# One merge's PSUM bank: chunk 2's 16-row blocks take the first bank of the feed-forward sums

## The chip, the cores and the metric

The kernel runs on one core of one Trainium2 chip. The metric is the device time of one execution in microseconds (us), and the number given for a kernel is the median of its runs. TensorE (PE; its weight loads are PEld), VectorE (DVE), ScalarE (ACT) and GpSimd (POOL) each work through their own instructions in order. SyncE (SP) starts the transfers. PSUM, into which TensorE writes, has eight banks, and this kernel uses all eight while the attention runs.

## What is computed

The reference runs a recurrence over 768 time steps and then two gated feed-forward layers over all 3072 tokens of width 320. Cut to what matters:

```python
for t in range(S):                                   # S = 768, 4 batches x 8 heads, D = 40
    y[:, :, t] = einsum('bhd,bhde->bhe', rt, state)
    Sa = einsum('bhde,bhe->bhd', state, at)
    state = state * wt[:, :, None, :] - einsum('bhd,bhe->bhde', Sa, bt) + einsum('bhd,bhe->bhde', vt, kt)
x = y.transpose(0, 2, 1, 3).reshape(3072, 320)
x = (silu(x @ w_gate) * (x @ w_val)) @ w_out         # first layer, d_ff = 1536
x = (sigmoid(x @ w_gate2) * (x @ w_val2)) @ w_out2   # second layer
```

## The kernel before, in words

The recurrence is cut into 12 chunks of 64 steps. Within a chunk it becomes matrix work: products of the decayed keys, the inverse of a unit triangular matrix for each of 32 head and batch pairs, and a few products that carry the state from chunk to chunk. Each chunk m passes through these stages.

- `prep_a(m)` loads and scales the inputs, transposes them (`tr4`, L371) and makes four key products `kps` (L486), each in the bank "mm" for every chunk but 0. ScalarE takes the triangle `bn` out of `kps` (L495, L496), VectorE takes the masked rest `lq` (L498), and only then is the bank free for the next `kps`.
- `prep_b(m)` inverts the triangle. For chunks below `FEW = 3` it calls `halves` (L546): VectorE solves blocks of 16 rows (L567, L573) and transposes them (L578, L579); then TensorE merges pairs of them into blocks of 32 rows, in a PSUM tile `hps` (L588, L601), with a copy by ScalarE between the two (L596) and copies behind them (L615, L617, L619). From chunk 3 on it calls `whole` (L510): VectorE solves blocks of 32 rows by itself (L520, L521, L526, L532, L536) and a transfer through DRAM turns them. Both kinds end in the last merge, from 32 to 64 rows: `zps` and `xps` (L647) with their copies (L664, L662). The result is `X`.
- `chain(m)` carries the state: `qps` (L692 or L766), `ups` (L710 or L787, which needs `X`), `sps` (L723 or L811). For chunks 0 to 2 it runs in two halves of eight pairs, the first in the bank "qu", the second in "zy".
- `post(m)` makes the outputs: `aps` (L861), masked by VectorE (L870), and `yps` (L892), read by VectorE (L906), all of them in "zy".
- `extra(m)` runs block m of the first feed-forward layer: `split` (L1058 to L1074), `gate` into the bank "gv" (L1112), and sums into the two banks "po0" and "po1" (L1128), which ScalarE copies out (L1383).

The eight banks are two of "tp" (transposes) and one each of "zy", "qu", "gv", "mm", "po0" and "po1". A tile with a tag waits until the tile that had the tag before is read for the last time. The merges of chunk 0 and 1 (`hps`, `zps`, `xps`) have "po0" and "po1", those of all later chunks have "mm", the same bank as `kps`.

The order of the work is made in two steps. A function `merge` (L920) interleaves the stages of several chunks by written costs and due times: beside each other run `chain` and `post` of chunk m, `prep_b` of chunk m + 1, `prep_a` of chunk m + 2, the feed-forward block m - 1, and the splitting of feed-forward weights into two parts (`load_w`, L1000 to L1038, work of all engines but TensorE). Then the framework, when the kernel is built, orders the instructions of each engine by a timed plan: earlier in the program has priority, and an instruction whose tile has no free bank yet stands back. On the chip each engine keeps that order.

Two SBUF buffers matter as well. `halves` and `whole` share the tag "pr", of which there is one: in chunk 2 it holds `zt`, which ScalarE writes at L596 and TensorE reads at L601; in chunk 3 it holds `nt` (L520), the first step of the solve. The tag "sn", also one, is free by then.

After the attention the remaining feed-forward work runs as a stream on TensorE (`gates`, L1167, and `add`, L1128).

Of the kernel before, what the change touches and what calls it, by code (L numbers as in the profile page):

```python
# [24 lines left out]
FEW = 3  # L25
# [17 lines left out]
def attention(ctx, tc, st, ident, ins, banks, extra, early, more):  # L43
# [75 lines left out]
    def tied(mats, gates):  # L119
        for x, ys, c in [(mats[0], gates, "Sync"), *((x, mats[:1], "NoSync") for x in mats[1:])]:  # L120
            for y in ys:
                tc.add_manual_dep(
                    x.ins,
                    y.ins.name,
                    mybir.DependencyInfo(getattr(mybir.DependencyClass, c), mybir.DependencyReason.DATA),
                    reason="one group",
                )
# [89 lines left out]
    ptp, pzy, pqu, pmm, po = banks()  # L217
# [406 lines left out]
    def prep_b(m):  # L624
        X = xinv[m % 2]
        while m not in inv:
            yield
        bn = inv.pop(m)
        pool, tag = (po, f"po{m}") if m < 2 else (pmm, "mm")
        if m < FEW:  # L630
            ps = pool.tile([P, NS, 32], F32, tag=tag, name="hps")
            steps = halves(m, X, bn, ps)
        else:
            steps = whole(m, X, bn)
        for x1t in steps:
            yield

        zt = wk.tile([P, NS, 32], F32, tag="zt", name="zt")
        for n in range(2):
            ps = pool.tile([P, NS, 32], F32, tag=tag, name="zx"[n] + "ps")  # L640
            mats = []
            for q in range(NS):
                for h2 in range(2):
                    with group(m, not mats):
                        lo, hi = slice(64 * h2, 64 * h2 + 32), slice(64 * h2 + 32, 64 * h2 + 64)
                        mats.append(
                            nc.tensor.matmul(  # L647
                                ps[(hi, lo)[n], q],
                                lhsT=(bn[lo, q, 32:64], zt[hi, q])[n],
                                rhs=(x1t[lo, :, q], X[hi, q, 32:64])[n],  # L650
                                start=True,
                                stop=True,
                                tile_position=(64 * h2 + 32 * n, 64 * h2 + 32 - 32 * n),
                            )
                        )
            if m >= FEW:
                tied(mats, copied if n else [])
            copied = []
            for h2 in range(2):
                lo, hi = slice(64 * h2, 64 * h2 + 32), slice(64 * h2 + 32, 64 * h2 + 64)  # L660
                if n:
                    nc.scalar.mul(out=X[lo, :, 32:64], in_=ps[lo], mul=-1.0)  # L662
                else:
                    copied.append(nc.scalar.copy(out=zt[hi], in_=ps[hi]))  # L664
            yield
        if m == 0:
            marks["merged"] = mats[-1]

    def group(m, first):
        return tc.high_priority(2000) if m >= FEW and not first else nullcontext()  # L670
# [278 lines left out]
    for t, step in ((x16, 17), (xs, 34)):  # L949
        t = t.rearrange("p r t -> p (r t)")[:, ::step]  # L950
        nc.gpsimd.tensor_copy(out=t, in_=odd[:, 0:1].to_broadcast([P, 16]) if step == 34 else less.to_broadcast([P, 16]))
    nc.gpsimd.memset(tkb[2][..., D:64], 0.0)
    start = [(prep_b(0), *QB)]
    if NCH > 1:
        start.append((prep_a(1), *QA))
    merge(start)
    for m in range(NCH + 1):
        todo = []
        if m == 0:
            todo.append((early(range(NFA - 2)), *QW))  # L960
            if len(groups) > 1:
                todo.append((all_powers(), *QP))
        if m == 1:
            todo.append((early(range(NFA - 2, NFA), lambda x: behind(x, "late")), *NL))
        if 0 <= m < NCH:
            todo.append((cp(m), *(NP if m else QN)))
        if 0 <= m < NCH - 1:
            todo.append((prep_b(m + 1), *(NB if m else QC)))
        if 2 <= m + 2 < NCH:
            todo.append((prep_a(m + 2), *(NA if m else QD)))  # L970
        todo.append((ahead(m), *(NX if m > 1 else (QX, NF1)[m])))
        if more is not None:

            free = {NCH - 2: [f"lq{NCH % 3}", f"tkb{NCH % 3}"]}
            free[NCH - 1] = [f"lq{(NCH + 1) % 3}", f"tkb{(NCH + 1) % 3}", "part0"]
            free[NCH] = ["part1", f"lq{(NCH + 2) % 3}", "part3", f"tkb{(NCH + 2) % 3}", "ut", "rbd", "part2"]
            todo.append((more(free.get(m, []), (raw_of(wk, ("zt", "x1t")), (pmm, "mm")) if m >= NCH - 1 else None), *NM))
        merge(todo)
# [578 lines left out]
```

## Time and profile before

| | |
|---|---|
| median of 3 runs | 1272.05 us (1271.22 to 1274.35) |
| profiled execution, its own time | 1274.74 us |
| span of its profile, first to last instruction | 1272.7 us |
| TensorE busy | 1185.2 us, 93% |
| VectorE busy | 687.8 us, 54% |
| ScalarE busy | 592.3 us, 47% |
| GpSimd busy | 557.7 us, 44% |
| mean granted TensorE clock | 0.956 of full speed |

The profile is one execution. Its own time is 2.7 us above the median of the runs, and 2.0 us of it lie outside the span. A timeline row names start, duration, engine, line, operation, the tile written and the tiles read, and in brackets how long the engine was idle before it and whose end it waited for. Names are those of the program; "part" stands for tensors that are parts of shared buffers (`X`, `an`, `mask`, the state). The clock of TensorE has two levels here, 2.4 GHz (1.00) and 1.2 GHz (0.50); a number between them is a mean over a stretch with both. Matmuls of 32-bit numbers count as two records each.

### The profile page before, as it was taken

How to read it: one execution, taken by the hardware profiler on the slowest of the kernel's cores; microseconds unless marked ns; L12 is line 12 of the kernel's file. 1: busy time of each engine (PE TensorE's matmuls, PEld its weight loads, DVE VectorE, ACT ScalarE, POOL GpSimd, SP SyncE). 2: the span in 40 equal slices, each digit the busy share in tenths (PEclk: the TensorE clock that was granted, in tenths of full speed). 3: DMA queues.
4: the chain of work that ended last, by engine and by line, in shares of the span. 5: the costliest groups of instructions: out<-in, count | busy, mean ns of one | idle time of the engine just before them, and what ended most of it. 6: DMA issues, size and time to landing. Idle time of an engine off the chain costs nothing.

```text
span 1272.7 us, 31392 instructions
## 1 busy us (share of the span) xinstructions
PE 1185.2 (93%) x12545; PEld 1070.1 (84%) x12545; DVE 687.8 (54%) x1432; ACT 592.3 (47%) x1447; POOL 557.7 (44%) x749
## 2 busy tenths in 40 slices
PE   5598799999999999899999999999999999999997
PEld 4487588889889988788898888888888888888886
DVE  6867769876678667956867544467121212121111
ACT  8465546556655575455433433445232323232222
POOL 5744842233223224356855766676232223222221
PEclk8678868999999999999999999999999999999998
DMA  7444664544655555343464543323010101000001
GB/s 221 131 131 148 146 168 123 123 99 111 153 121 115 115 136 122 88 106 110 125 237 126 182 160 127 107 88 91 2 46 1 46 1 35 1 21 1 22 1 25
DMA packets 180460, 124.38 MB, mean 98 GB/s; under 512 B 134608, under 2 KB 160208, under 8 KB 179536
## 3 DMA queue, kind: packets, MB, share of 16 engines
q1 hardware_dynamic: 180144, 122.11, 35.5%
q8 instruction: 101, 1.65, 0.5%
q14 instruction: 55, 0.45, 0.1%
q10 hardware_dynamic: 160, 0.16, 0.1%
HBM read 90.81 MB, written 31.43 MB: 96 GB/s over the span
## 4 chain that ended last, share of the span: by engine, by line
PE 60%; DVE 22%; ACT 8%; issue 4%; DMA 2%; POOL 2%; SPq 0%; DVEq 0%; ACTq 0%; POOLq 0%
PE g L1167 31%; PE po L1128 16%; DVE pr L526 4%; PE gv L1112 4%; DVE part L532 3%; PE kps L486 2%; PE aps L861 2%; PE tp L371 2%; DVE lq L498 1%; PE ups L787 1%; ACT bn L496 1%; DVE am L870 1%; DVE dt L1015 1%; ACT bn L495 1%; ACT part L751 1%
## 5 line engine op out<-in xcount | busy, mean ns | idle before, releaser
L1167 PE MATMUL g<-x,w 128*128 128x512 f32 (+1 forms) x1792 | 419.8, 385 | 2.1 <-DVE g L1174 2.0
L1167 PEld LDWEIGHTS g<-x,w 128*128 128x128 f32 x1792 | 323.3, 188 | 62.8 <-issue 2.8
L1176 POOL TENSOR_TENSOR hl<-g,hh 128x256 fp32r<-128x256 f32 x216 | 162.1, 756 | 281.8 <-ACT hh L1175 253.9
L1174 DVE TENSOR_TENSOR g<-g,g 128x256 f32<-128x256 f32 x216 | 82.1, 419 | 342.4 <-PE g L1167 340.1
L1128 PE MATMUL po<-w,hh 128*128 128x320 f32 x1152 | 233.6, 311 | 0.9 <-ACT hh L1118 0.8
L1128 PEld LDWEIGHTS po<-w,hh 128*128 128x128 f32 x1152 | 187.0, 188 | 9.9 <-ACT hh L1118 1.0
L1175 ACT CAST hh<-g 128x256 fp32r<-128x256 f32 x216 | 86.9, 406 | 179.4 <-PE po L1128 169.7
L1112 PE MATMUL gv<-x,w 128*128 128x256 f32 x1152 | 165.6, 291 | 3.8 <-DVE g L1117 2.5
L1128 PE MATMUL po<-w,hl 128*128 128x320 f32 x576 | 151.1, 313 | 3.6 <-POOL hl L1119 3.5
L1112 PEld LDWEIGHTS gv<-x,w 128*128 128x128 f32 x1152 | 147.7, 192 | 6.8 <-DVE g L1117 3.9
L1171 ACT ACTIVATE g<-g 128x256 f32<-128x256 f32 x216 | 73.0, 382 | 149.5 <-PE g L1167 143.1
L1119 POOL TENSOR_TENSOR hl<-g,hh 128x256 fp32r<-128x256 f32 x72 | 62.8, 872 | 128.8 <-ACT hh L1118 127.9
L1032 POOL TENSOR_TENSOR dt<-dt,w 128x384 f32<-128x384 f32 (+1 forms) x72 | 80.3, 1116 | 87.5 <-ACT w L1030 42.7
L1128 PEld LDWEIGHTS po<-w,hl 128*128 128x128 f32 x576 | 99.6, 188 | 5.6 <-POOL hl L1119 5.2
L498 DVE TENSOR_TENSOR lq<-kps,part 64x256 f32<-64x256 f32 x96 | 40.5, 422 | 85.9 <-ACT bn L496 67.0
L526 DVE TENSOR_TENSOR pr<-part,sn 128x4 f32<-128x4 f32 (+4 forms) x135 | 76.2, 565 | 3.7
L1014 DVE TENSOR_SCALAR dt<-dt 128x384 int32<-128x384 int32 (+1 forms) x72 | 41.8, 580 | 52.8 <-POOL dt L1011 52.5
L486 PE MATMUL kps<-lq,kbt 104*128 104x128 f32 x384 | 61.3, 309 | 8.9 <-DVE lq L498 6.4
L532 DVE TENSOR_REDUCE part<-pr 128x2 f32<-128x4 f32 (+4 forms) x135 | 66.6, 493 | 2.8
L486 PEld LDWEIGHTS kps<-lq,kbt 104*128 104x128 f32 x384 | 53.4, 215 | 13.2 <-PE yps L892 4.1
L861 PE MATMUL aps<-rbd,ut 104*128 104x128 f32 x384 | 57.1, 295 | 6.1 <-DVE ysb L906 3.6
L1030 ACT CAST w<-dt 128x384 fp32r<-128x384 f32 (+1 forms) x72 | 35.6, 495 | 55.3 <-DVE dt L1015 48.2
(185 smaller groups left out, 1711.4 us busy)
## 6 DMA issues: line engine op xcount, KB each, us to landing
raw<-in_w_dram SPq DMA_DIRECT2D x48, 384.0 KB
xd<-x SPq DMA_DIRECT2D x12, 896.0 KB
x<-xd SPq DMA_DIRECT2D x11, 896.0 KB
raw<-in_w_dram SPq DMA_DIRECT2D x24, 320.0 KB
ld<-in_a_kb_dram SPq DMA_DIRECT2D x22, 320.0 KB
ld<-rd SPq DMA_DIRECT2D x64, 80.0 KB
pn<-pd SPq DMA_DIRECT2D x32, 160.0 KB
ld<-in_a_a_dram SPq DMA_DIRECT2D x12, 320.0 KB
```

What stands on the lines that cost most here:

```text
L486: nc.tensor.matmul(kps[:, n].rearrange("p h t -> p (h t)"), lhsT=kbt[0:PW, n, :], rhs=lq[m % 3][0:PW, 4 * g4 + n].rearrange("p h t -> p (h ...
L526: nc.vector.tensor_tensor(out=o, in0=xs[:, 0:kk, None, 0:n].to_broadcast([P, kk, 2, n]), in1=sn[:, None, n : n + 2, 0:n].to_broadcast([P, ...
L532: nc.vector.tensor_reduce(out=xs[:, 0:kk, n : n + 2], in_=o, axis=AX.X, op=ALU.add)
L861: nc.tensor.matmul(aps[:, n, h2], lhsT=ut[0:PW, x, 2 * h2 : 2 * h2 + 2].rearrange("p u s -> p (u s)"), rhs=rbd[0:PW, x, h2].rearrange("p b ...
L1032: sub(out=tf, in0=tf, in1=w.bitcast(F32), op=ALU.subtract)
L1112: nc.tensor.matmul(gv[n], lhsT=p, rhs=q, start=e == 0, stop=e == len(seq) - 1)
L1128: self.nc.tensor.matmul(ops[u], lhsT=p[:, us], rhs=q, start=first and n == 0, stop=last and n == 2)
L1167: nc.tensor.matmul(gv[k][:, 0:n], lhsT=p, rhs=cols(at), start=e == 0, stop=e == len(seq) - 1)
L1171: nc.scalar.activation(out=g[j], in_=gv[0][:, j], func=AF.Silu if silu else AF.Sigmoid)
L1174: nc.vector.tensor_tensor(out=g[j], in0=gv[1][:, j], in1=g[j], op=ALU.mult)
L1175: nc.scalar.copy(out=hh, in_=g[j])
L1176: self.heng.tensor_tensor(out=hl, in0=g[j], in1=hh.bitcast(F32), op=ALU.subtract)
```

## The change

For chunk 2 the tiles `hps`, `zps` and `xps` get the tag "po0" in place of "mm". For chunks 0 and 1 the tag is what it was ("po0", "po1"), and from chunk 3 on too ("mm"). No instruction is added, removed or altered in size.

```diff
@@ -626,7 +626,7 @@
         while m not in inv:
             yield
         bn = inv.pop(m)
-        pool, tag = (po, f"po{m}") if m < 2 else (pmm, "mm")
+        pool, tag = (po, f"po{m % 2}") if m < FEW else (pmm, "mm")
         if m < FEW:
             ps = pool.tile([P, NS, 32], F32, tag=tag, name="hps")
             steps = halves(m, X, bn, ps)
```

## Rows read from the trace of the kernel before

**Rows 1.** The page: TensorE's granted clock in 40 slices of 31.8 us, tenths.

```profile
PEclk8678868999999999999999999999999999999998
```

**Rows 2.** Windows: stretch, us, busy of PE, PEld, DVE, ACT, POOL, clock, DMA share, GB/s.

```profile
152.00:165.00 13.00, 10.63 (x68) 9.42 (x69) 5.75 (x10) 8.06 (x20) 8.09 (x11) 0.52 0.93 233
165.00:174.00 9.00, 7.04 (x220) 6.69 (x219) 5.22 (x12) 6.11 (x14) 3.01 (x4) 0.88 0.30 103
174.00:201.00 27.00, 26.49 (x438) 24.02 (x437) 21.44 (x48) 10.54 (x24) 11.96 (x17) 0.51 0.67 166
201.00:245.90 44.90, 42.32 (x695) 38.73 (x695) 41.29 (x78) 27.67 (x68) 12.81 (x15) 1.00 0.42 99
244.30:288.00 43.70, 40.55 (x674) 37.87 (x674) 32.57 (x65) 25.77 (x63) 12.49 (x15) 1.00 0.54 123
329.60:371.20 41.60, 40.17 (x672) 37.69 (x671) 30.97 (x64) 25.29 (x63) 12.26 (x15) 1.00 0.53 121
...
454.50:496.20 41.70, 40.25 (x674) 37.78 (x673) 31.06 (x64) 25.37 (x63) 12.33 (x15) 1.00 0.49 112
```

**Rows 3.** PE timeline, chunk 3's key products and chunk 2's merge.

```profile
146.60 1.16 PE L486 MATMUL kps<-lq,kbt 104*128 104x128 f32 x8
...
167.41 1.06 PE L486 MATMUL kps<-lq,kbt 104*128 104x128 f32 x8
...
171.67 1.26 PE L588 MATMUL hps<-x1t,bn 16*32 16x16 f32 x128 [1.06 <-DVE lq L498]
...
179.75 1.05 PE L601 MATMUL hps<-part,pr 32*16 32x16 f32 x102
...
189.25 1.92 PE L647 MATMUL xps<-part,zt 32*32 32x32 f32 x64
...
193.72 2.08 PE L486 MATMUL kps<-lq,kbt 104*128 104x128 f32 x8 [0.51 <-ACT part L662]
```

**Rows 4.** DVE timeline, chunk 2's blocks, then the solves of chunks 3 and 4.

```profile
138.45 0.70 DVE L578 STREAM_TRANSPOSE x1t<-x 128x512 f32<-128x512 f32 x1
...
172.97 0.61 DVE L906 TENSOR_TENSOR ysb<-yps,pn 128x320 f32<-128x320 f32 x2
...
180.92 0.85 DVE L617 TENSOR_SCALAR part<-hps 16x256 f32<-16x256 f32 x2 [0.37 <-PE hps L601]
181.80 0.69 DVE L520 TENSOR_TENSOR nt<-sn 128x512 f32<-128x512 f32 x1
182.41 0.70 DVE L619 STREAM_TRANSPOSE x1t<-part 128x512 f32<-128x512 f32 x1
...
211.28 0.71 DVE L536 STREAM_TRANSPOSE x1t<-part 128x512 f32<-128x512 f32 x1
...
218.47 1.23 DVE L512 STREAM_TRANSPOSE sn<-bn 128x1024 f32<-128x1024 f32 x1
```

**Rows 5.** Windows, columns as in Rows 2: from the end of L906 on.

```profile
173.58:181.80 8.22, 7.96 (x164) 6.97 (x164) 3.97 (x9) 1.65 (x3) 4.70 (x7) 0.50 0.52 125
...
173.60:245.90 72.30, 68.98 (x1132) 62.91 (x1133) 62.73 (x125) 38.20 (x91) 25.17 (x33) 0.81 0.51 123
...
173.60:211.30 37.70, 36.11 (x561) 32.67 (x562) 31.54 (x64) 17.77 (x44) 14.15 (x21) 0.64 0.54 136
```

**Rows 6.** ACT timeline: po0 copied out, and chunk 4's keys ready.

```profile
144.44 0.43 ACT L1383 COPY ob<-po 128x320 f32<-128x320 f32 x1
...
176.94 0.59 ACT L482 COPY kbt<-tp 104x512 f32<-104x512 f32 x1 [0.94 <-PE tp L371]
```

**Rows 7.** PE timeline: chunk 1's merge in its own bank, between chunk 2's key products.

```profile
106.05 1.16 PE L486 MATMUL kps<-lq,kbt 104*128 104x128 f32 x8
...
108.72 1.27 PE L588 MATMUL hps<-x1t,bn 16*32 16x16 f32 x128
...
120.57 1.25 PE L647 MATMUL xps<-part,zt 32*32 32x32 f32 x64
...
122.96 1.16 PE L486 MATMUL kps<-lq,kbt 104*128 104x128 f32 x8 [1.14 <-DVE lq L498]
```

## The prediction

> **What bounds the kernel now.** The table of the page says that TensorE is busy for 93% of the span. I read its clock by slices next: it is 9 tenths and more from the eighth slice (223 us) to the end, but 6 tenths in the sixth (159 to 191 us) [rows 1]. The windows by stage say more. The chunk windows are cut at the starts of `ups` (L787). From chunk 4 on a chunk takes 41.6 to 41.7 us, of which TensorE is busy 40.2 at full clock; chunk 3's stretch takes 43.7 with 40.55 [rows 2]. So TensorE bounds the later chunks, a shift of the work before them is kept to the end, and what this change can win lies between 140 and 246 us. Before that, 152 to 165 us runs at a clock of 0.52 and 174 to 201 us at 0.51, almost wholly at 1.2 GHz [rows 2].
>
> The timelines show what holds that stretch. The blocks of chunk 2 are solved and transposed (L578) at 139.15 us [rows 4], yet their merge starts at 171.67, 32.5 us later, and the row names the reader of a key product, L498, as what it waited for [rows 3]. That is the shared bank: the four products of chunk 3 pass through "mm" from 146.60 to 168.5 us, and the merge gets it behind the last of them. Behind the merge's last copy, L662, the first product of chunk 4 starts at 193.72 [rows 3], though its keys were ready at 177.5 us (176.94 + 0.59 [rows 6]). So the bank makes each wait for the other, once in each direction.
>
> On VectorE I read the solves. The solve of chunk 3 goes from L520 at 181.80 to the end of L536 at 211.99 [rows 4]. Its first result `nt` has the buffer of chunk 2's `zt`, which L601 reads until 180.80 [rows 3]; VectorE itself was past L906 at 173.58 [rows 4]. The solve of chunk 4 starts with L512 at 218.47, once chunk 4's four products are read [rows 4], and ends with the stretch that I cut at 245.9. VectorE is busy 62.73 of the 72.30 us from 173.6 to 245.9 [rows 5], and TensorE 68.98, much of that at half clock. Both are near their limit there, with VectorE's solves as the longest chain.
>
> **What the change moves.** It takes nothing away and adds nothing: the merge's matmuls, copies and transposes stay as they are. What changes is what they wait for.
>
> *The start of the merge.* "po0" is free once block 0's first sum is copied out, at 144.87 us (144.44 + 0.43 [rows 6]). So the merge can start at about 145 in place of 171.67, 26.8 us earlier. Chunk 1 shows the same merge in a bank of its own beside key products: L588 at 108.72, xps done at 121.82, 13.1 us [rows 7]. From 145 that gives an end at about 158; before it was 191.17 [rows 3]. `X` of chunk 2 is then ready before its chain wants it.
>
> *The added wait on "po0".* On TensorE the merge now stands behind L1383 of block 0; behind it are the transposes and chunk 3's key products. TensorE has idle time there (2.4 us of 13 in the next window [rows 2]), which covers a stall of an instruction or two; without that cover it would cost TensorE what L1383 is late. Block 1's sums now wait for the read of xps. They come after the old end of the merge even if the merge does not move, so this costs 0 while the merge ends before 190 us or so. The seven ScalarE copies of the merge come among chunk 3's evictions instead of behind them. In chunk 1's case the four products took 16.9 us between their starts (106.05 to 122.96 [rows 7]) with a merge among them; chunk 3's took 20.8 us without one (146.60 to 167.41 [rows 3]). So I cost this at nothing. If ScalarE's idle time (13 - 8.06 us [rows 2]) fails as a cover, seven copies of at most the 0.59 us of L482 [rows 6], 4.1 us, delay chunk 3's triangle; that is the bound.
>
> *The solve of chunk 3.* L520 can start right behind L906 at 173.58 instead of 181.80: 8.22 us earlier. Those 8.22 us were not empty. VectorE was busy for 3.97 of them with other work [rows 5], which has still to be done, so 4.25 us were idle. Of the merge itself, L617 (0.85) and L619 (0.70) leave for VectorE's idle time before 165 us (5.75 busy of 13 [rows 2]). Gain on VectorE: 4.25 + 0.85 + 0.70 = 5.8 us.
>
> *The solve of chunk 4.* The first product of chunk 4 can go at 178 instead of 193.72, so chunk 4's triangle no longer comes last and its solve can follow chunk 3's at once. How much idle time of VectorE that closes is not shown. The upper end: all idle time from 173.6 to 245.9 goes, 72.30 - 62.73 = 9.57 [rows 5], and with L617 and L619 11.1 us. The lower end is the 5.8, and 0 if VectorE's order keeps L520 where it is. I take the middle of 5.8 and 11.1, **8.4 us**, since the other waits in that stretch (for TensorE, for ScalarE's activations) remain in part.
>
> *TensorE's share.* Can it follow? From 173.6 to 211.3 it is idle 37.70 - 36.11 = 1.59 us [rows 5], and L601's last part, xps and zps leave it: 1.05 + 1.92 [rows 3] and, for zps, which has as many matmuls of the same shape, another 1.92, or 4.9 us. From 201 to 245.9 it is idle 2.58 [rows 2]. Together some 9 us at the same clock, so TensorE allows 8.4, just.
>
> *The rest.* From 246 us on TensorE is busy 40.2 of 41.6 us in each chunk, so the shift stays. What is late next is TensorE itself.
>
> **The sum.** The profiled execution took 1274.74 us; less 8.4 that is 1266.3. The profile is 2.7 us above the median of the runs, 1272.05; from the median, 1272.05 - 8.4 = **1263.6 us**.
>
> The clock is the large unknown. The rows show both levels: the same eight records of L486 take 1.06 us at 167.41 and 2.08 at 193.72, and the clock fell between the stretch to 174 us (0.88) and the next (0.51), behind the tiny matmuls of L588 [rows 2, 3]. If the merge's leaving lets it stay at 2.4 GHz from 174 to 201, 26.49 us of work could shrink by up to 13.2 us, and VectorE would be the bound.
>
> The Trainium skill, page "TensorE: Matmul & The Clock Gate", section "Terms", prices a throttled stretch as its length times one minus the share of clock: 40 us (13 + 27) would be worth 20 us, an estimate, and the sum by it alone 1252; here no row shows the stretch unthrottled.
>
> **Rivals.**
>
> *A, the clock holds as well.* For it: the solve and the chain are then held by VectorE alone (11.1 us at most from 173.6 on), and chunk 3's products come at chunk 1's pace, 16.9 instead of 20.8 us, 3.9 us more. That gives 15 us: 1257. Against it: the clock already fell at 152 us, before any merge.
>
> *B, no change that can be measured.* The merge moves, but its tiny matmuls bring the low clock into 145 to 174 us, where it is 0.88 from 165 on: 7.04 us of work there [rows 2] could take some 6 us more, and 8.4 - 6 = 2.4 is left: 1269.6. For it: behind the first L588 the clock fell. The Trainium skill, same page, section "A second HAM failure mode: psum-queue depth-cycling", says that short idle times between groups of matmuls that cycle through PSUM banks make the clock go back and forth; the trace's two falls agree. Against: in chunk 1 xps was at full pace 12 us behind L588 (1.25 us [rows 7] against 1.92 [rows 3]). Also in B: the plan made at the build leaves the merge behind chunk 3's products, so that the change does little; then 1270 to 1272. Against that: the wait for L498 is stated in the row.
>
> *C, slower.* The place is chunks 4 to 10. The plan of all later work is laid out anew when the bank changes, and a chunk may fall into chunk 3's pattern of 43.7 us instead of 41.6, 2.1 us each. It decides from four chunks on (8.4 / 2.1); in all seven it costs 14.7, so 6.3 us net: 1278. For it: one stretch has that pattern now. Against: that one follows directly on the disturbed start, and those behind it hold 41.6 to 41.7 [rows 2].
>
> **How the numbers follow.** My forecast, 4 to 13 us faster (1259 to 1268), has 0.48; A 0.17; B 0.21; C 0.14. A measurement tells 0.3%, 3.8 us, from no change. Faster: 0.48 + 0.17 = 0.65; same 0.21; slower 0.14. The range from 1253 to 1274 takes in A down to 19 us and B up to 2 us slower; it leaves out C and the extreme of A.
>
> **What would show it.** Right: L588 of chunk 2 between 144 and 150 us, with L1383 as its releaser or none; L520 of chunk 3 at 173 to 175; the first product of chunk 4 at about 178, no longer behind L662; the end of chunk 4's solve at 236 to 239; chunk 4's stretch and the later ones 41.6 us. Wrong: L520 still behind 180; the low clock from 145 on; a period above 42.5 us; or a wait of L1128 for L662 of chunk 2.

## The result, and the profile after

The changed kernel is slower: 1284.29 us (median of 20 runs, 1272.96 to 1296.71) against 1273.18 for the kernel before on the same chip (20 runs, 1270.93 to 1276.23). The ratio is 1.0085, with a 95% interval of 1.0066 to 1.0104. It leaves out two runs of the changed kernel, 1294.48 and 1296.71, which count as slow. The profiled execution of the changed kernel took 1290.89 us, its span 1289.1; that is 6.6 us above its median, so differences of single profiles are read below by stretches. A second profile of the changed kernel (run 7, 1289.15 us) stands beside it; both are slower than 15 of the 20 runs, and what its fastest run, 1272.96 us, did differently was not seen.

Cut both spans where chunk 3's and chunk 9's first `ups` (L787) start: before 244.33, 251.77 and 776.6 us; after 246.55, 264.66 and 777.9. So 2.2 us were lost in the start, 12.9 in the six chunks from there, 1.3 behind them; together 16.4, the difference of the spans (1289.1 - 1272.7).

**The start.** TensorE's clock by slices in the page of the changed kernel (the answer to [rows 1]), then the windows of the first stretch (columns as in [rows 2]):

```profile
PEclk8677759999988989999999999999999999999999
```

```profile
140.00:152.00 12.00, 9.41 (x200) 7.56 (x201) 7.28 (x14) 8.13 (x19) 7.31 (x11) 0.82 0.87 212
152.00:165.00 13.00, 11.78 (x218) 10.17 (x217) 5.85 (x13) 8.16 (x21) 7.46 (x10) 0.50 0.89 223
165.00:174.00 9.00, 9.00 (x106) 8.04 (x106) 3.97 (x9) 5.40 (x12) 1.63 (x3) 0.50 0.34 111
174.00:201.00 27.00, 25.84 (x379) 23.37 (x376) 16.68 (x43) 14.43 (x35) 9.95 (x14) 0.66 0.47 107
201.00:246.55 45.55, 41.06 (x587) 38.35 (x587) 42.39 (x82) 25.56 (x63) 18.65 (x21) 0.96 0.54 137
```

TensorE is busy almost throughout from 152 to 174 us (20.78 of 22.00 us), but at 0.50, that is 1.2 GHz; the merge's own matmuls (the end of L588, L601, `zps`) are 4.0 us of it, the rest is other work at half rate. From 165 to 174 it was 0.88 before [rows 2]. The next slices below 9 tenths lie among the later chunks, where before none did [rows 1].

TensorE's timeline of the changed kernel, chunk 2's merge and chunk 3's key products (compare [rows 3]):

```profile
144.82 0.75 PE L588 MATMUL hps<-x1t,bn 16*32 16x16 f32 x66
146.34 0.33 PE L588 MATMUL hps<-x1t,bn 16*32 16x16 f32 x17
148.32 0.30 PE L588 MATMUL hps<-x1t,bn 16*32 16x16 f32 x7 [1.65 <-issue]
148.55 2.08 PE L486 MATMUL kps<-lq,kbt 104*128 104x128 f32 x8
...
156.43 1.92 PE L486 MATMUL kps<-lq,kbt 104*128 104x128 f32 x8
158.27 1.26 PE L601 MATMUL hps<-part,pr 32*16 32x16 f32 x128
165.43 1.91 PE L486 MATMUL kps<-lq,kbt 104*128 104x128 f32 x8
...
174.69 2.08 PE L486 MATMUL kps<-lq,kbt 104*128 104x128 f32 x8
178.99 1.92 PE L647 MATMUL xps<-part,zt 32*32 32x32 f32 x64
```

VectorE's timeline of the changed kernel, where chunk 3's solve begins and where it ends (compare [rows 4]):

```profile
177.49 0.43 DVE L498 TENSOR_TENSOR lq<-kps,part 64x256 f32<-64x256 f32 x1 [4.45 <-ACT bn L496]
...
180.00 1.23 DVE L512 STREAM_TRANSPOSE sn<-bn 128x1024 f32<-128x1024 f32 x1
181.26 0.94 DVE L520 TENSOR_TENSOR nt<-sn 128x512 f32<-128x512 f32 x1
...
222.47 0.69 DVE L536 STREAM_TRANSPOSE x1t<-part 128x512 f32<-128x512 f32 x1
223.09 0.64 DVE L520 TENSOR_TENSOR nt<-sn 128x512 f32<-128x512 f32 x1
```

The merge did move: L588 starts at 144.82 in place of 171.67, xps 10.3 us earlier. But the last key product starts 7.3 us later, so the triangle is transposed (L512) at 180.00, and L520 gains 0.5 us instead of 8.2. The solve then takes 41.9 us to 223.16, where before it took 30.2. Two things stand between its steps: more of VectorE's other work (18.5 us of it, before 10.7) and more idle time (6.5 us, before 1.9), of which 3.24 are one wait for `aps` (L861) of TensorE, still at half rate. Chunk 4's solve starts 3.2 us later than before (223.09 against 219.94).

**The six chunks.** Windows of these in the kernel before, then in the changed one; below the changed one's, three of its chunks (before, these three took 41.6 to 41.7 us each, at 1.00 [rows 2]):

```profile
244.33:496.10 251.77, 241.39 (x4015) 226.35 (x4014) 187.48 (x380) 152.15 (x373) 73.82 (x85) 1.00 0.53 122
```

```profile
246.55:511.21 264.66, 249.13 (x4015) 233.90 (x4014) 190.16 (x382) 153.25 (x374) 68.53 (x85) 0.96 0.51 115
331.49:376.82 45.33, 41.93 (x670) 39.77 (x669) 30.89 (x63) 25.64 (x63) 11.06 (x14) 0.92 0.53 131
376.82:423.01 46.19, 43.56 (x670) 40.45 (x669) 32.02 (x63) 25.35 (x63) 11.44 (x14) 0.93 0.46 99
423.01:467.96 44.95, 42.72 (x671) 40.54 (x670) 30.90 (x63) 25.64 (x63) 11.05 (x14) 0.92 0.55 130
```

TensorE runs the same 4015 matmuls. It is idle 15.53 us instead of 10.38, and the matmuls take 7.74 us longer at a clock of 0.96: 5.15 + 7.74 = 12.9. Against the periods of before (43.55 and five of 41.6 to 41.7) the six chunks changed by -0.8, +0.5, +3.7, +4.6, +3.3 and +1.6 us. The waits say where the idle time comes from. First TensorE in the changed kernel (line, what it waited for, us in total, times, longest), then ScalarE:

```profile
PE kps L486 <- DVE lq L498: 7.5, 5, 3.3
PE po L1128 <- ACT hh L1118: 6.6, 4, 2.5
```

```profile
ACT ob L1383 <- DMA xs<-ob: 7.7, 4, 2.8
```

Before, TensorE waited 2.6 us for L498 in those chunks, never 0.2 us or more for L1118, and ScalarE's L1383 not once for its transfer. One such place, on ScalarE and then on TensorE:

```profile
361.43 0.43 ACT L1383 COPY ob<-po 128x320 f32<-128x320 f32 x1 [1.52 <-PE po L1128]
...
363.15 0.59 ACT L482 COPY kbt<-tp 104x512 f32<-104x512 f32 x1
366.54 0.43 ACT L1383 COPY ob<-po 128x320 f32<-128x320 f32 x1 [2.80 <-DMA xs<-ob]
366.99 0.38 ACT L495 ACTIVATE bn<-kps 32x256 f32<-32x256 f32 x1
```

```profile
368.24 2.05 PE L486 MATMUL kps<-lq,kbt 104*128 104x128 f32 x8 [3.33 <-DVE lq L498]
370.08 0.85 PE L1058 MATMUL xtp<-ident,ysb 128*128 128x128 f32 x3
370.86 3.06 PE L766 MATMUL qps<-part,lq 128*64 128x40 f32 x64
```

A block's sums leave through one buffer, `ob`, in two halves. The second copy waits until the first half is sent; the reader of a key product (L495) stands behind it on ScalarE, so TensorE runs dry for 3.33 us and goes on at half rate (L486 2.05 us instead of 1.06 to 1.16). In the kernel before, the two copies of that block ran without a wait:

```profile
360.34 0.43 ACT L1383 COPY ob<-po 128x320 f32<-128x320 f32 x1
...
363.83 0.43 ACT L1383 COPY ob<-po 128x320 f32<-128x320 f32 x1
```

There ScalarE came to the second copy 3.07 us after the end of the first (3.06 to 3.08 in all six chunks). In the changed order it comes to it at 363.74, the end of L482, 1.88 us after the end of the first, and the buffer is free only after 4.7 us; at the other such place, in the chunk of 44.95 us, after 1.88 and 3.5. So 1.2 us of each of these two waits come from copies that stand closer together, the rest from a transfer that was done later than 3.07 us after its copy.

A second kind of place is in the chunk of 46.19 us, in which no copy waits. VectorE's multiply L1117 stands there behind steps of the solve (405.65, right behind an L532), and L1128 waits for L1118, which reads its result; in the last chunk, of 43.25 us, the same wait takes 1.72 us.

```profile
406.56 0.94 PE L1128 MATMUL po<-w,hh 128*128 128x320 f32 x4 [2.51 <-ACT hh L1118]
```

### The profile page after: what moved, and what is told of

Its sections match the earlier page's. It is cut to its first block, busy times and chain, and to the rows that moved or that the text cites. A ratio compares the mean times of both kernels' runs of the same rounds, so it can differ in the third digit from the quotient of the medians.

```text
span 1289.1 us, 31427 instructions
## 1 busy us (share of the span) xinstructions
PE 1200.8 (93%) x12545; PEld 1085.3 (84%) x12545; DVE 686.3 (53%) x1432; ACT 592.2 (46%) x1447; POOL 549.9 (43%) x749
## 4 chain that ended last, share of the span: by engine, by line
PE 69%; DVE 17%; issue 4%; DMA 3%; ACT 3%; POOL 2%; SPq 0%; POOLq 0%; ACTq 0%; DVEq 0%
PE g L1167 30%; PE po L1128 17%; PE gv L1112 6%; PE kps L486 3%; PE tp L371 3%; DVE pr L526 3%; DVE part L532 2%; PE aps L861 2%; DMA wt<-in_a_w_dram 2%; PE yps L892 1%; PE qps L766 1%; DMA xs<-ob 1%; PE xtp L1058 1%; DVE lq L498 1%; PE ups L787 1%
## 5 line engine op out<-in xcount | busy, mean ns | idle before, releaser
L1176 POOL TENSOR_TENSOR hl<-g,hh 128x256 fp32r<-128x256 f32 x216 | 162.5, 756 | 294.9 <-ACT hh L1175 275.9
L1128 PE MATMUL po<-w,hh 128*128 128x320 f32 x1152 | 236.0, 312 | 10.4 <-ACT hh L1118 10.3
L1128 PEld LDWEIGHTS po<-w,hh 128*128 128x128 f32 x1152 | 188.2, 189 | 20.4 <-ACT hh L1118 11.5
L1128 PE MATMUL po<-w,hl 128*128 128x320 f32 x576 | 154.5, 316 | 1.1 <-POOL hl L1119 0.9
L1119 POOL TENSOR_TENSOR hl<-g,hh 128x256 fp32r<-128x256 f32 x72 | 56.3, 784 | 119.9 <-ACT hh L1118 119.5
L1128 PEld LDWEIGHTS po<-w,hl 128*128 128x128 f32 x576 | 100.2, 189 | 4.6 <-POOL hl L1119 4.0
L498 DVE TENSOR_TENSOR lq<-kps,part 64x256 f32<-64x256 f32 x96 | 40.5, 422 | 81.6 <-ACT bn L496 80.1
L486 PE MATMUL kps<-lq,kbt 104*128 104x128 f32 x384 | 66.9, 329 | 12.9 <-DVE lq L498 10.0
L526 DVE TENSOR_TENSOR pr<-part,sn 128x4 f32<-128x4 f32 (+4 forms) x135 | 72.9, 540 | 3.7
L486 PEld LDWEIGHTS kps<-lq,kbt 104*128 104x128 f32 x384 | 58.9, 234 | 16.8 <-issue 7.3
L532 DVE TENSOR_REDUCE part<-pr 128x2 f32<-128x4 f32 (+4 forms) x135 | 66.5, 493 | 3.0
L861 PE MATMUL aps<-rbd,ut 104*128 104x128 f32 x384 | 59.5, 304 | 6.9 <-DVE am L870 2.5
L861 PEld LDWEIGHTS aps<-rbd,ut 104*128 104x128 f32 x384 | 53.2, 213 | 9.9 <-issue 4.6
```

What stands on the lines that cost most here:

```text
L486: nc.tensor.matmul(kps[:, n].rearrange("p h t -> p (h t)"), lhsT=kbt[0:PW, n, :], rhs=lq[m % 3][0:PW, 4 * g4 + n].rearrange("p h t -> p (h ...
L526: nc.vector.tensor_tensor(out=o, in0=xs[:, 0:kk, None, 0:n].to_broadcast([P, kk, 2, n]), in1=sn[:, None, n : n + 2, 0:n].to_broadcast([P, ...
L532: nc.vector.tensor_reduce(out=xs[:, 0:kk, n : n + 2], in_=o, axis=AX.X, op=ALU.add)
L861: nc.tensor.matmul(aps[:, n, h2], lhsT=ut[0:PW, x, 2 * h2 : 2 * h2 + 2].rearrange("p u s -> p (u s)"), rhs=rbd[0:PW, x, h2].rearrange("p b ...
L1128: self.nc.tensor.matmul(ops[u], lhsT=p[:, us], rhs=q, start=first and n == 0, stop=last and n == 2)
L1176: self.heng.tensor_tensor(out=hl, in0=g[j], in1=hh.bitcast(F32), op=ALU.subtract)
```

## Experiments

Theory 1: most of the loss lies behind 246 us, in the new order of the later chunks, where the second copy of a block's sums waits. Theory 2: the loss is made before 246 us by the early merge and the low clock, and only carried on. The tables of stretches below are taken like the three numbers above: start, six chunks, rest.

**1. The merge held back, in its new bank.**

```diff
+ if m == 3 and g4 == 3: marks["products"] = last      # L486, chunk 3's last key product
+ if m == 2: behind(first, "products")                 # L588, chunk 2's merge
```

> The changed kernel, with the merge of chunk 2 (L588) ordered on TensorE behind the last key product of chunk 3, where it stood before; its bank stays po0. The engines' order from chunk 5 on is then nearly the one of the kernel before. Theory 1 (most of the loss lies behind 246 us, in the new order of the later chunks, where the second copy of a block's sums waits on ScalarE for the transfer of the first): the periods from chunk 4 on are 41.6 to 41.7 us again, and the start is like before or a little better, since chunk 4's key products no longer wait for the merge: 1266 to 1272 us. Theory 2 (the loss is made before 246 us, by the early merge and the low clock it brings, and only carried on): also back to 1268 to 1273, with the solve of chunk 3 at about 181 us.

1269.07 us, ratio 0.9984 (0.9968 to 0.9999). Stretches 241.19, 249.74 and 773.8. The bank as such does no harm, and the slow periods are gone; but their order is gone as well, so this alone does not tell the theories apart.

**2. The merge held back behind the second product only** (`g4 == 1` in the same edit).

> The changed kernel, with the merge of chunk 2 ordered behind the second key product of chunk 3, half way between its two places. The engines' order from chunk 5 on is that of the changed kernel. Theory 1: the periods of chunks 4 to 8 are 43 to 46 us as in the changed kernel, and the time is 1279 to 1288 us whatever the start gives. Theory 2: the merge disturbs less of the start, so the time comes down to 1273 to 1279.

1290.59 us, ratio 1.0139 (1.0121 to 1.0156), above the ranges of both theories. Stretches 246.33, 264.67, 778.4. TensorE's order is that of the changed kernel from the end of the start on, and the six chunks cost the same to 0.01 us, with 7.4 us of waits of the copy for its transfer.

**3. Two outgoing buffers in the changed kernel,** paid for with one buffer of `ysb`. **4. The same in the kernel before,** as a control.

```diff
- ysb = wk.tile([P, DM + 64], F32, tag="ysb", name="ysb", bufs=3)
+ ysb = wk.tile([P, DM + 64], F32, tag="ysb", name="ysb", bufs=2)
- ob = h_p.tile([P, DM], F32, tag="ob", name="ob", bufs=1)
+ ob = h_p.tile([P, DM], F32, tag="ob", name="ob", bufs=2)
```

> The changed kernel, with two buffers for the copied sums (ob) in place of one; to make room, ysb has two in place of three, which by itself alters no engine's order. The order of the later chunks is laid out anew by this. Theory 1: the second copy waits for no transfer, the periods of chunks 5 to 7 fall from 45 to 46 us to under 43, and the time to 1270 to 1277 us. Theory 2: the start is the changed kernel's (chunk 3's ups at 246 us or later), and the time stays at 1281 to 1287 us.

> The kernel before with the same two buffers for ob and two for ysb: the control for the run with two buffers. Theory 1: the copies of the kernel before wait little for transfers (6.8 us in all over its profile), so 1268 to 1274 us. Theory 2: the same.

The changed kernel came to 1271.4 us, ratio 0.9988 (0.9971 to 1.0005), stretches 241.47, 250.03, 778.2, with no wait of the copy. The control missed: 1280.54, ratio 1.0058 (1.0044 to 1.0072), stretches 248.16, 254.34, 777.0. From chunk 4 on its chunks run steadily at 41.65 us, but the start is laid out anew and slower, and chunk 3's takes 46.1. So an edit of two buffer counts moved the time by 8 us by the plan alone, and what follows keeps the order or compares stretches.

**5. The first half of a block sent twice in the kernel before; 9. sent seven times.** A dose of the wait, in before's order of TensorE, VectorE and GpSimd.

```diff
+ if u == 0 and 1 < m < 9:
+     nc.sync.dma_start(out=xs2, in_=ob)        # 9: six times
  nc.sync.dma_start(out=xs[1][2 * m + u], in_=ob)
```

> Edit: the kernel before, and for blocks 2 to 8 the first half of the block's output is sent a second time, to a scratch buffer, before the single buffer of outgoing sums comes free. The order of TensorE, VectorE, ScalarE and GpSimd is that of before; only the sync engine issues seven more transfers. It is a dose of the suspected wait, given where the plan is not laid out anew. Theory 1 (the later chunks lose because ScalarE's second copy of a block's sums waits for the transfer of the first, TensorE runs dry behind it and its clock falls): the chunk periods from 330 to 550 us rise from 41.65 to 43.5 to 46, the copy's rows name the transfer, the granted clock of those chunks is 0.90 to 0.96, and the whole comes to 1283 to 1300. Theory 2 (the loss lies before 246 us, the wait is hidden): periods stay 41.6 to 42.0, the whole 1271 to 1276.

> Edit: as the kernel with the first half sent twice, but sent seven times in all for blocks 2 to 8, since one more transfer made no wait. The order on TensorE, VectorE and GpSimd is that of before. Theory 1 (a second copy that waits for the buffer runs TensorE dry and turns its clock down): ScalarE's second copy waits 2 us or more for the transfers, the chunk periods between 283 and 500 us rise from 41.65 to 43.5 to 46 and the granted clock there falls below 0.97; the whole 1282 to 1300. Theory 2 (such a wait is hidden in the later chunks): the wait is there, but periods stay 41.6 to 42.0, the whole 1268 to 1276. If no wait arises, the run tells nothing.

Sent twice: 1271.79 us, ratio 1.0001 (0.9979 to 1.0023). No copy waited in the six chunks, so the dose was too small and the run says nothing. Sent seven times: 1292.23 us, ratio 1.014 (1.0106 to 1.0174); stretches 243.59, 275.44, 777.7. ScalarE's waits for transfers in its six chunks and what TensorE waited for most, then two of the copies and what stood behind them, and windows of three chunks:

```profile
ACT ob L1384 <- DMA xs<-ob: 15.8, 5, 4.9
```

```profile
PE tp L371 <- ACT part L755: 12.4, 5, 4.5
```

```profile
348.49 0.43 ACT L1384 COPY ob<-po 128x320 f32<-128x320 f32 x1 [4.89 <-DMA xs<-ob]
348.81 0.43 ACT L755 COPY part<-tp 104x320 f32<-104x320 f32 x1
...
391.62 0.43 ACT L1384 COPY ob<-po 128x320 f32<-128x320 f32 x1 [3.53 <-DMA xs<-ob]
391.95 0.43 ACT L755 COPY part<-tp 104x320 f32<-104x320 f32 x1
```

```profile
336.06:381.45 45.39, 40.75 (x670) 37.74 (x669) 30.89 (x64) 25.35 (x63) 12.26 (x15) 1.00 0.55 134
381.45:428.46 47.01, 41.64 (x670) 39.14 (x670) 31.33 (x64) 25.43 (x63) 12.31 (x15) 0.96 0.54 136
471.23:519.03 47.80, 42.90 (x671) 40.36 (x670) 31.34 (x64) 25.43 (x63) 12.31 (x15) 0.93 0.48 119
```

TensorE, VectorE and GpSimd keep before's order here; ScalarE does not: the second copy of a block stands 21 to 23 us behind the first (348.49 behind 325.26, 391.62 behind 370.35) in place of 3.5, with L755 behind it. TensorE is idle 14.2 us more than before in the six chunks, and its waits for L755 (12.4 us, before 2.6) and for the copies themselves (3.2 us, before none) make 13.0 of them. Four chunks with a waiting copy took 45 to 48 us; one, with a wait of 2.3 us, took 42.8, and the first took 47.0 without one. In the first of the three shown the clock stayed at 1.00 and the chunk still cost 3.7 us more: the idle time is the first cost, and the lower clock comes on top where it falls. The six extra transfers also load the queue; what that adds this run does not separate.

**6. The changed kernel with the buffer free at once.**

```diff
- nc.sync.dma_start(out=xs[1][2 * m + u], in_=ob)
+ sent = x[:, 0:DM].bitcast(F32) if u == 0 and 1 < m < 9 else ob
+ nc.sync.dma_start(out=xs[1][2 * m + u], in_=sent)
```

**7. The changed kernel again,** unedited, on the same chip as run 6.

> Edit: the changed kernel, but for blocks 2 to 8 the transfer of the first half takes its bytes from a buffer that nobody waits for, so the outgoing buffer is free at once (the first halves of those seven blocks' outputs hold other data). The order of the work is that of the changed kernel but for a dozen places on ScalarE. Theory 1: the wait of the second copy for the transfer is gone; the periods of 45.3 and 45.0 us between 331 and 468 come down to 42 to 43.5; what is left is VectorE's multiply behind the solve (the period of 46.2); the whole 1275 to 1281. Theory 2: periods as in the changed kernel, the whole 1284 to 1291.

> The changed kernel once more, unedited, for a second profile of it. Theory 1: the loss in the later chunks comes from short waits that turn the clock down or not, so it differs from execution to execution: some periods between 246 and 550 us are 44 to 46 and others 41.7 to 42.5, not all in the same chunks as in the first profile; the start of chunk 3's stretch is at 241 to 248; runs spread over 10 us and more. Theory 2: the loss is made before 246 us and alike in each: start of chunk 3's stretch at 246 to 248 and the same periods within 0.3 us as in the first profile.

With the buffer free (the first halves of blocks 2 to 8 then hold other data): 1276.47 us, ratio 1.0045 (1.0013 to 1.0077). Again unedited: 1290.67, the median of 4 runs, ratio 1.0146 (1.0112 to 1.018); the first 20 runs had 1284.29. So 7.8 to 14.2 us lie between two kernels with the same order on TensorE, VectorE and GpSimd. Stretches: 241.06, 254.62, 774.1 with the free buffer; 246.52, 262.42, 778.4 unedited. The profile with the free buffer is the fastest of its ten runs, 5.0 us below their median, and its start lies before the first transfer that the edit alters; the six chunks are what it tells of. The six chunks in the windows of the first, and three of its chunks:

```profile
241.06:495.68 254.62, 242.79 (x4015) 227.76 (x4015) 189.89 (x382) 153.38 (x374) 70.93 (x85) 0.99 0.52 119
```

```profile
326.03:367.15 41.12, 39.97 (x670) 37.79 (x669) 30.90 (x63) 25.66 (x63) 12.05 (x14) 1.00 0.55 127
367.15:410.55 43.40, 40.41 (x670) 37.75 (x669) 31.04 (x63) 25.45 (x63) 11.73 (x14) 1.00 0.52 118
410.55:451.67 41.12, 39.98 (x670) 37.80 (x669) 30.89 (x63) 25.65 (x63) 12.07 (x14) 1.00 0.55 127
```

The chunks that took 45.33 and 44.95 us take 41.12, and TensorE's busy time is back at 242.79. The chunk with L1117 behind the solve stays slow, 43.40, as theory 1 expected, and TensorE's waits for L1118 are still 6.2 us over the six chunks. That it took 2.8 us less than in the first profile is not the copy's doing in any way that the rows show: no copy had waited in it. Its wait for L1118 was 1.91 us in place of 2.51, and its clock 1.00 in place of 0.93. The repeat missed a part of its expectation: the slow periods lie in the same chunks as in the first profile (45.13, 44.52, 43.84), so the pattern belongs to the order, not to chance. Its start, 246.52 us, came as theory 2 had it; its periods differ from the first profile's by up to 1.7 us where theory 2 allowed 0.3.

**8. Merge held back and two buffers** (edits 1 and 3 together).

> Edit: the changed kernel with the merge of chunk 2 held behind chunk 3's last key product, and two outgoing buffers for a block's sums (paid for with one buffer of the feed-forward's input less). Both suspected causes are out. Theory 1: no wait of the second copy for the transfer, periods 41.6 to 41.8 from 283 us on, start of chunk 3's stretch at 241 to 243, the whole 1264 to 1270. Theory 2: the early stage alone counts: as the kernel with the merge held back alone, 1266 to 1272. If the plan of the first 250 us is laid out badly, as with two buffers in the kernel before, the start is at 246 to 249 and the whole 1275 to 1282.

1275.06 us, ratio 1.0026 (1.0001 to 1.0051), stretches 246.5, 254.74, 770.3. No wait of the copy, but a start as slow as the changed kernel's, and periods of 41.1 to 44.2 us where 41.6 to 41.8 were expected. It is not the best of both, and an order can be slow without that wait.

**10. The transfers issued by ScalarE in the changed kernel; 11. the same in the kernel before.**

```diff
- nc.sync.dma_start(out=xs[1][2 * m + u], in_=ob)
+ nc.scalar.dma_start(out=xs[1][2 * m + u], in_=ob)
```

> Edit: the changed kernel with the transfers of the first feed-forward's sums issued by ScalarE behind its own copy in place of the sync engine, where they stand behind loads of 1.7 to 4.2 us. All outputs are computed. The order on TensorE differs from the changed kernel's in 418 lines of some 9500 (from before's the changed kernel differs in 2138). Theory 1: the second copy waits under 1 us, the periods between 331 and 468 us come down from 44 to 46 to 41.7 to 43.5, the whole 1268 to 1279. Theory 2: periods and time as in the changed kernel, 1284 to 1291.

> Edit: the same move of the transfers to ScalarE in the kernel before, as a control. Theory 1: before has no such wait between 245 and 512 us, so nothing is to be won there: periods 41.6 to 41.8, the whole 1268 to 1276. Theory 2: if the queue matters on its own, it gains as much as in the changed kernel, 6 us or more: 1258 to 1266.

The changed kernel: 1276.75 us, ratio 1.0039 (1.0017 to 1.006); before: 1273.19, ratio 1.001 (0.999 to 1.0029). The second came as theory 1 had it. The first time is in the expected range for the wrong reason. The second copy still waits 8.2 us for its transfer, though each transfer is now issued within 0.1 us of its copy, so the sync engine's queue was not what made it late. The six chunks still take 264.11 us, but no row ties that to this wait. From chunk 3 on the order is a third one, and TensorE waits for L498 there nowhere for 0.2 us or more. Its waits name L906, 11.3 us, and L1118, 4.4 us; at each wait for L906 VectorE was busy with steps of the solve that its order puts first. One of them (ScalarE's total, TensorE's total, then VectorE's and TensorE's timelines):

```profile
ACT ob L1383 <- DMA xs<-ob: 8.2, 6, 2.0
```

```profile
PE xtp L1058 <- DVE ysb L906: 11.3, 6, 2.2
```

```profile
316.71 1.30 DVE L526 TENSOR_TENSOR pr<-part,sn 128x900 f32<-128x900 f32 x1
318.04 0.62 DVE L906 TENSOR_TENSOR ysb<-yps,pn 128x320 f32<-128x320 f32 x2
```

```profile
318.59 0.90 PE L1058 MATMUL xtp<-ident,ysb 128*128 128x128 f32 x3 [2.21 <-DVE ysb L906]
```

The gain lies in the start, 238.07 us, the shortest of all runs. TensorE's order there is that of the changed kernel; the clock is not (columns as before):

```profile
152.00:165.00 13.00, 12.38 (x245) 10.47 (x245) 6.75 (x14) 9.61 (x25) 8.68 (x11) 0.67 0.98 252
165.00:174.00 9.00, 8.48 (x205) 7.57 (x205) 4.73 (x10) 7.60 (x17) 3.23 (x5) 1.00 0.58 182
174.00:201.00 27.00, 24.07 (x367) 21.53 (x360) 24.67 (x58) 18.57 (x47) 13.82 (x18) 0.94 0.61 151
```

**12. Two buffers and ScalarE's transfers together** (edits 3 and 10).

> Edit: the changed kernel with two outgoing buffers (one buffer of the feed-forward's input less, as in the run with two buffers) and with ScalarE issuing the transfers. So far the time is a sum of three stretches: to the first state product of chunk 3 (238 to 248 us), from there six chunks on (250 to 255 us without the wait of the second copy, 262 to 275 with it), and the rest (770 to 778 us). Theory 1: with a second buffer there is no wait, so the six chunks take 250 to 255 us whoever issues the transfer; the first stretch is 238 to 247, by the clock that TensorE gets from 152 to 201 us; the whole 1262 to 1274. Theory 2 (the wait is not what counts, but the changed order): the six chunks take 260 us or more and the whole is 1276 or more.

1278.69 us, ratio 1.0055 (1.0034 to 1.0077): a miss in total. The start (241.5) and the six chunks (252.94, no wait of the copy) came as theory 1 said; the rest took 783.6, 5 us and more above the others; between 580 and 600 us TensorE was busy for 15.61 of 20 us, at 0.91. What held it there was not followed up.

**Taken together.** In the fourteen profiles, the six chunks take 262.4 to 275.4 us wherever the copy waited for its transfer for 6.4 us or more in them (the changed kernel twice, runs 2, 9 and 10), and 249.7 to 254.7 wherever it waited for 1.4 us or less. That count alone proves little: in run 10 TensorE's waits did not stand behind the copy at all. For the changed kernel theory 1 holds in part. Taking the wait away in its order (6) brings the two chunks in which TensorE stood behind the copy back to 41.12 us, and a wait added where TensorE's order is the old one (9) makes chunks slow. The two chunks of 46.19 and 43.25 us have by their rows another cause, VectorE's multiply behind the solve, which the new order brought and no run took away with the order kept. What stays open is why the transfer was done so late at the two places: it still came late with the issue moved to ScalarE (10), and the load of the transfers at that moment was not tested. For the start neither theory is enough: the same order took 246.5 us with 0.50 from 152 to 174, and 241.06 and 238.07 where the clock came back earlier. What turned it was not found.

## Why the prediction was wrong

- **"From 246 us on TensorE is busy 40.2 of 41.6 us in each chunk, so the shift stays" failed, and cost most.** It put the later chunks at no change, and the six became 12.9 us longer. TensorE bounded them only while the waits in them ended in time, as they did in the order of before. The two chunks with the wait of the copy lost 7.0 us, the two with L1117 behind the solve 6.2, and the first two together won 0.3. Free of the wait of the copy (6) the six take 254.62, 10.0 less than in the first profile and 7.8 less than in the second.
- **Rival C had the side and the place right, the mechanism not.** It priced a laid-out-anew plan at 2.1 us for each of seven chunks by chunk 3's pattern. In the changed kernel three chunks lost 3.3 to 4.6 us each, two by a copy waiting for a transfer, which it never did there in the kernel before, one by VectorE's multiply behind the solve. That C's 1278 lies within 7 us of the measured 1284.29 is luck. Its chance of 0.14 was too low: the text knew that all later work is laid out anew, and took the steadiness of one order as evidence about another.
- **"I cost this at nothing" failed.** With the merge among them the four key products took 26.1 us between their starts (148.55 to 174.69) instead of 20.8, 5.3 more and past the bound of 4.1. Chunk 1's 16.9 us was the wrong model: it ran beside other work and at a clock of 0.90, this one at 0.50. ScalarE's copies were not the limit; TensorE was busy 20.78 of the 22.00 us from 152 on, at half rate.
- **The solve of chunk 3 failed with it.** L520 came at 181.26, not 173.58. Its cause in before, the buffer held until the merge was over, was read right and went away; the triangle was late next. Even with the clock back (run 10) it came at 176.79.
- **The start of the merge was right, its length was not:** it began at 144.82 against "about 145", but xps ended at 180.91 and not at about 158, 36.1 us in place of chunk 1's 13.1. The first product of chunk 4 came at 188.99 and not behind L662, yet not at 178.
- **Rival B's sign was right for the start:** the low clock moved into 152 to 174 us. The size of 6 us for 165 to 174 is near the 7.3 us that the last key product lost. B still left 2.4 us of gain; the start came 2.2 us later. Rival A's start appeared too, in run 10: 6.3 us earlier than before in place of 15.

The Trainium skill, page "TensorE: Matmul & The Clock Gate", section "Terms", prices a throttled stretch as its length times one minus the share of clock. For the six chunks that makes 264.66 × 0.04 = 10.6 us, an estimate; the trace has 7.74 us of longer matmuls. The order of size agrees, but 5.15 us of idle time come beside it, which the rule does not count.

## What to carry to other kernels

Where instructions are laid out by a planner, a freed resource in one place is a new order everywhere behind it: compare the periods of later stages before trusting that a shift is kept, and give the new order a chance of its own to lose. A single buffer between a copy and its transfer is harmless only while the two copies stay apart by more than the transfer takes; look at what stands behind the second copy in its engine's queue. To test such a wait, take it away with the order kept, and follow whether the engine that bounds the stretch stands behind it: in run 10 the copy waited as long, and TensorE did not.

## What was not expected of the hardware

The same order on TensorE took its start in 246.5 us (twice), 241.06 and 238.07, with the clock of 165 to 174 us at 0.50, 0.50, 0.71 and 1.00. TensorE was 94% to 100% busy in those 9 us each time, so the low level there stood beside a busy engine, not an idle one. The changed kernel's 20 runs spread over 23.8 us where those of before spread over 5.3; that this start is the reason was not shown. A waiting copy alone, at a clock of 1.00, still cost 3.7 us in a chunk.
